# Query and key transposes of two batches moved from TensorE to the DMA crossbar, with paced loads, smaller V loads, a last block in halves and a newly searched plan

## The chip, the cores and the metric

The kernel runs on one core of one Trainium2 chip. The metric is device time in microseconds (us) per execution, as the median of several executions; lower is better. A profile is one execution with every instruction recorded; its span is some 2 us shorter than the time (188.3 against 190.54 us in the kernel before). TensorE (PE) multiplies matrices, VectorE (DVE) and ScalarE (ACT) work element by element, GpSimd (POOL) here makes masks and issues the loads that cast to bf16 ("software" DMA queue), and SyncE (SP) issues all other transfers ("hardware" queue; the page of before has 12896 packets in the one and 43256 in the other).

## The reference

Four batches of attention with eight heads of 64 over 768 positions, each followed by a "wave" layer on the joined heads (512 wide).

```python
# attention: 3 heads causal, 5 "streaming" (4 sink keys and a window of 64)
scores = np.matmul(q, k.transpose(0, 1, 3, 2)) / np.sqrt(D)
a = softmax(np.where(mask, scores, -1e9))
x = np.matmul(a, v)                     # heads joined: [4, 768, 512]
# wave layer
theta = x @ w_theta
y = w_tok_r @ (x * cos(theta)) + w_tok_i @ (x * sin(theta))   # mixes the 768 positions
u = x + y
out = u + np.maximum(u @ w_ch, 0)
```

The kernel lays out every product with its contracted axis on the 128 partitions (the rows of the on-chip memory), so it transposes q and k before the scores, x before theta, and u before the last product. The DMA crossbar, named often below, transposes a block while it is being transferred (DMA_TRANSPOSE in the traces; a block of x, 128x512, lands 2.4 us after issue in the median of before).

## The kernel before

All work is a list of small steps, each with an engine, a duration, what it waits for and which buffer it takes. A scheduler in the kernel plays the list as a plan when the program is built. A step's rank in the plan is corrected by a number from a long list, `TILT`, which a search has tuned; the plan's order is then the fixed order of instructions on each engine. The plan of before already has x (after the first batch) and u (all but the last block) transposed by the DMA crossbar, issued from SP, while q and k are transposed on TensorE:

```python
def turn_qk(what, b, n):                 # 12 transposes of 128x64 into one PSUM bank
    pt = state["pt", what, n] = mine_bf()
    for j in range(NB):
        for x, h in enumerate(PAIRS[n]):
            nc.tensor.transpose(pt[64*x:64*x+64, j*128:(j+1)*128], state[what, b][:, h, j*D:(j+1)*D], ident)

def keep_qk(what, n):                    # the copy out of PSUM, strided, on VectorE or ScalarE
    dst = (qT if what == "q" else kT)[n]
    copy(dst.rearrange("d (p j) -> d p j", j=NB), state.pop(("pt", what, n))[:, :S].rearrange("d (j p) -> d p j", j=NB))

def send_x(b, i):                        # already by crossbar, issued from SP
    nc.sync.dma_start_transpose(state["xT", b][:, :, i*128:(i+1)*128], state["x", b][:, i])
# ... cut: send_u is alike; store, load_v and move_v are plain transfers, also from SP
```

The softmax here doesn't subtract the row's maximum and nothing guards it: scores larger than these inputs give would overflow.

Of the kernel before, what the change touches and what calls it, by code (L numbers as in the profile page):

```python
# [25 lines left out]
    71383, 33577, 73294, -468, 272, 1817, 2121, 1841, 1484, 998, -351, -458, -9998906, -4244, 10993, 53854, -3405,  # L26
    6928, 42937, -27592, 3470, 440, -1170, -8668, 30584, 1187, 131611, 11003, 41350974, 22079, 7061, 59467, 66431,
    42364, 66838, 49232, 30363, 39667, 30343, 71323, 34095, 32360, 33997, 32661, 1599, -643, 481689, -687, 479643,
    10008299, 117742521, 135319420, 117742203, 135320132, 117742437, 135319441, 33665, 30756, 33818, 32757, 33944,
    32167, 96740665, 96740841, 96741207, 96740837, 96740995, -40086, 2489, -29404, 1496, 21511, 2417553, 21872,  # L30
    2417414, 1232, 23224485, 19914, 2417541, 36373805, 2417413, 41478, 20144064, 41910, 7510594, -1006, 10008162,
    27019, 10008687, 2317, -822, 71, 885, 30746, 4782, 28260, -700, 0, 851, 30200, 1234, 16671, -417, 8, -563,
    150, -315, 119, -744, 0, -2086, 0, 548, 3112, 184, 1256, -1791, 0, 218, 752, 196, 3175, -1205, 0, 71357, 6153,
    0, 32543, 49107, 31384, 1227, 34083, 31606, 41910, 2709, 478753, 42322, 1021, 20513511, 10009579, 33487,
    32376, 10009719, 3061386, 20516550, 22990, 135320173, 30384, 2419544, 52082, 68040, 33791, 31401, 59232,
    65497, 71091, 33781, 31241, 33656, 31212, 42036, 19480, 2416926, 79160287, 135318358, 36388668, 9882286,
    36359654, 9867371, 36386091, 9881900, 36360748, 9867822, 36380489, 9885853, 36359579, 16622892, 36360622,
    16626254, 36361168, 16622969, 36361066, 16623202, 4404, 16351, 59586, 28353, 4287, 16466, 36361251, 53261,
    16623326, 16375, 27903, 27573, 27919, 27740, 4295, 4300, 16459, 2029, 29794, 30117, 29643, 30164, 4475, -856,
    24, -2541, 30238, 13762, 8711, 13664, 36359955, 9868033, 53378, 28516, 4917, 16623645, 4811, 16623892, 7, 810,  # L40
    -2223, 740, 30630, 137, 686, 2190, 658, 5916, 2615, 6222, 0, 8869, 3362, -1287, 0, -358, -620, -1072, 378,
    -1088, 358, -1482, 0, -908, 3108, 3053, 2556, 3175, 1994, -541, 4029, -2027, 443, 3087, 6247, 7224, 7707,
    3524, 1446, 145, 28321, -1758, 3046, 3213, 1938, -265, 9029, 2043, 3371, 1753, 3145, 1901, 3091, 5532, 2593,
    3883, -1311, 3122, 3196, 1921, -469, 3313, 2509, -288, 569, 2781, 3713, 9243, 7431, 1470, 0, -192, 3831, 2019,
    0, 952, 2262, 2765, 1417, 4943, 2862, 3017, 627, 4671, 2631, 1041, 6646, 4670, 830, 1866, 27, 4080, 5248,
    5671, 6705, 5103, 5667, 5732, 5378, 7798, 3719, 5937, 5989, 4277, 5669, 5648, 5767, 10067, 15, 5805, 6197,
    3753, 6052, 4214, 4158, 27275, 4065, 3679, 484, 76, 699, 0, 8188, 2442, -2323, 3242, -771, 336, 0, 417, 3878,
    502, 6390, 0, 6397, 0, -201, -390, 2653, -1, 2536, 1439, 0, 27303, 4094, -1220, 699, 571, -377, 0, -2008,
    -550, 489, 1174, 4261, -521, 0, 2334, 3007, 3186, 357, 0, 539, 0, 381, 1594, 769, 681, -1176, 2403, 0, 1644,
    1424, 4167, 4774, -640, 3694, 4115, 1590, 52, 0, 10207, 10302, 17, 5487, 2487, 3322, 3685, 1958, -115, 0,  # L50
    1278, 435, 48, 4630, -7, 1570, 41, 4926, 2732, 2867, 316, -65, 3820, 5940, 46, 5714, -87, 4029, 6008, -900, 0,
    207, 3181, -1890, 0, 372, 425, 2534, 0, 2651, 0, 2938, 7089, 5815, 3035, 4150, -1419, 3038, 4396, -900, 4748,
    3928, 2180, -198, 4640, 4240, -232, 6156, 6885, 5623, 13470, 2411, 1320, 13077, 2453, 2898, 7265, 2931, 3846,
    2887, 7384, 303, 4693, 4266, 2983, 2820, 7808, 332, 2714, 7985, 7738, 3942, 2085, 7081, 13673, 1381, 1001, 97,
    13671, 1776, 2404, 0, 5385, 1277, 2572, 1913, 5381, 904, 2631, 0, 8668, 2704, -145, 1307, 12055, 2019, 142,
    1807, 2720, 2655, 1600, 11967, 4387, 5544, 4391, 5600, 4716, 3728, 2582, 1586, 1908, 1795, 1896, 2095, 3728,
    4504, 11880, 11792, 7607, 1480, 6181, -150, 2513, 3028, 3771, -520, 0, -904, 0, 1201, -1294, 774, 512, 5429,
    1558, 0, 4756, 4685, 3735, -27, 0, 1552, 0, 1212, 347, 0, 2223, 7107, 183, 0, -58, 525, 2032, 6140, 0, -349,
    0, 4456, 229, 3887, 3367, 1689, -826, 0, 13058, 12693, 2337, -246, 1411, -277, 787, 626, -2065, 0, 160, 1199,
    10944, 0, 566, 672, 136, 3705, 10380, 15055, 8015, -17, -1058, 0, 3989, 2971, 1172, 7388, -1070, 0, -401,  # L60
    1423, -2036, 0, 69, 7506, -199, -504, 1956, 8487, 284, 1558, -1901, 622, 1946, 496, 4131, -680, 1961, 7942,
    283, 1343, -1901, 2642, 0, 2935, 2901, -904, 0, 1807, 1884, 661, 0, 1498, 0, 8019, -368, -1831, 6187, 1508,
    13580, 7853, 1348, 13206, 5432, 3571, 1546, 14303, 6167, 1616, 13539, 8035, -553, 887, 6033, 3284, 1481, 8104,
    -515, 7983, -35, 5380, 3520, 4327, 2710, 14882, 4300, -225, 17476, 8037, -229, -2170, 8078, -355, -251, 5364,
    3027, 17524, 37247, 1593, 30869, 0, 37555, 1626, 31594, 0, 22131, 16141, 30282, 0, 21805, 16036, 30305, 41,
    4508, 977, 226, 1349, 2832, 1057, 18, 51, 2854, 2844, 89, 586, 8778, 8244, 8472, 4657, 2899, 2748, -123, -320,
    2283, 2087, 2174, 2098, 1672, 830, -790, -660, 5071, 4133, 3088, 3855, 7423, 7062, 9000, -975, -2753, 3331,
    5493, 1307, 31137, 0, 7964, 7870, 5312, 965, 29975, 54853, 5490, 15749, -619, 0, 587, 9022, 6186, 31738,
    30293, 285, 3736, 15797, -632, 0, 4912, 1715, -342, 1335, -509, 1610, 2359, -3159, -23, 0, 5374, 4362, 4287,
    16854, -304, 53, 2629, 2970, 285, 0, 4350, -993, 1817, 5218, -757, 1251, 2672, -1073, 1792, 0, 2872, 2629,  # L70
    2714, -1232, 767, 0, -1425, 1125, 2390, 0, 4905, 2655, -1663, -651, 2319, 3164, 28456, 141, 20332, 0, 2632,
    2284, -2379, 1034, 2273, 4363, 27747, 1034, 21235, 0, -669, 764, 12072, -454, 19612, 25792, 28797, 881, 21566,
    2456, 28301, 29807, 31171, 921, 30773, 934, 1327, 2527, 20772, 571, 28258, 1526, 1729, 1013, 679, -1128, 2221,
    2979, 21483, 744,
# [3 lines left out]
class Step:  # L78
# [7 lines left out]
    def __init__(self, on, fn, after, take, give, mode, bias, port, share):  # L86
        self.on, self.fn, self.after = on, fn, [a for a in after if a is not None]
        self.take, self.give, self.mode, self.bias, self.port, self.share = take, list(give), mode, bias, port, share
        self.eng = next(iter(on)) if len(on) == 1 else None
        self.users = 0  # L90
        self.slot = self.start = self.end = self.ns = None


class Plan:
# [18 lines left out]
    def add(self, on, ns, fn, after=(), take=None, give=(), mode=None, bias=0, port=False, share=None):  # L113
        s = Step(on if isinstance(on, dict) else {on: ns}, fn, after, take, give, mode, bias, port, share)
        for g in s.give:
            g.users += 1
        self.steps.append(s)
        return s

    def order(self, free):  # L120
# [8 lines left out]
        for s in reversed(self.steps):  # L129
            far = max(self.LATENCY[e][0] for e in s.on)  # L130
            near = min(self.LATENCY[e][1] for e in s.on)
            rank[s.n] = min(s.on.values()) + max((rank[n.n] + (near if len(s.on) == 1 and n.on.keys() == s.on.keys() else far) for n in later[s.n]), default=0)
# [24 lines left out]
        while events:  # L157
# [10 lines left out]
            for e in engines:  # L168
# [34 lines left out]
                if s.share:  # L203
                    o = "DMA" if e == "DMAH" else "DMAH"
                    rest = max(0, free.get(o, 0) - t) + sum(n.on[o] for n in ready.get(o, ()) if ready_at[n.n].get(o, 0) <= t)
                    ns += min(rest, ns * s.share) * (1 - 1 / s.share)
# [5 lines left out]
                far, near = self.LATENCY[e]  # L212
                heapq.heappush(events, (s.end, count, None))
# [19 lines left out]
def kernel(  # L233
# [40 lines left out]
    half_pi = const.tile([128, 1], F32, name="half_pi")  # L274

# [42 lines left out]
    def mine_bf():  # L318
        return mine().bitcast(BF16)
# [41 lines left out]

    def load_v(b, half):
# [627 lines left out]
```

## Time and profile before

| kernel before | |
|---|---|
| time, median of the first three runs | 190.54 us (190.36 to 191.03) |
| profiled span, granted TensorE clock | 188.3 us, 1.00 |
| TensorE busy, of it idle matmuls that fill gaps | 180.1 us, 6.7 us |
| TensorE idle from 0 to 30, 30 to 140, 140 us to the end | 3.8, 0.0, 4.4 us |

The prediction below shows the page and the table by stretches. The columns of a timeline are start, duration, engine and line, operation, destination and source, and how many like it in a row. A duration on SP is the time that SP stands at handing the transfers over, not the transfer: those of x land 2.4 us after issue in the median.

```profile
64.24 2.63 SPq L568 DMA_TRANSPOSE xT<-x  x2
66.96 0.54 SPq L632 DMA_DIRECT2D out_dram<-ot  x1
67.59 4.47 SPq L568 DMA_TRANSPOSE xT<-x  x3
72.11 0.57 SPq L632 DMA_DIRECT2D out_dram<-ot  x1
72.78 1.23 SPq L568 DMA_TRANSPOSE xT<-x  x1
```

These are the six transposes of the second batch's x. One is handed over in 1.2 to 1.5 us, a store in about 0.55, and one follows the other: between 64.24 and 74.01 us SP stands still for less than 0.4 us.

### The profile page before, as it was taken

To read this page: it belongs to the slowest core of one execution; us is meant where nothing else is said; L and a number is where in the kernel's file an instruction comes from. 1 tells how busy PE (TensorE), PEld (TensorE's weight loads), DVE (VectorE), ACT (ScalarE), POOL (GpSimd) and SP (SyncE) were. 2 spreads that over 40 slices of the span, in tenths; PEclk is the share of its full clock that TensorE was granted. 3 is DMA by queue.
4 is the path that set the end of the run, shared out by engine and by line. 5 is a ranking of instruction groups with operands and counts; after the bars stand their busy time and mean duration, and the time that the engine had idled before them with its cause. 6 is when DMAs were issued, how large, how long until landed. Compare 5 with 4: busy or idle time off the path is not lost.

```text
span 188.3 us, 5126 instructions
## 1 busy us (share of the span) xinstructions
PE 180.1 (96%) x2143; PEld 101.2 (54%) x2143; DVE 130.7 (69%) x250; ACT 103.9 (55%) x129; POOL 60.0 (32%) x131
## 2 busy tenths in 40 slices
PE   6699989999999999999999999999999999999982
PEld 6546687764545874454447366444346564444430
DVE  7757696999855986997446466997249259935451
ACT  4488856698777707575780449686860356400010
POOL 7889878109737200005570020500320100000000
PEclk9999999999999999999999999999999999999999
DMA  5999999999999995978999952242344523234323
GB/s 175 173 188 205 200 206 204 208 207 222 147 234 274 196 136 139 209 158 187 181 128 228 104 159 41 61 95 111 87 111 58 168 59 79 61 120 106 108 111 113
DMA packets 56174, 28.06 MB, mean 149 GB/s; under 512 B 40408, under 2 KB 53080, under 8 KB 56152
## 3 DMA queue, kind: packets, MB, share of 16 engines
q1 hardware_dynamic: 43256, 17.65, 43.5%
q0 software_dynamic: 12896, 10.09, 36.1%
q8 instruction: 16, 0.26, 0.6%
q14 instruction: 6, 0.05, 0.1%
HBM read 25.71 MB, written 6.29 MB: 170 GB/s over the span
## 4 chain that ended last, share of the span: by engine, by line
PE 90%; DMA 3%; DVE 3%; ACT 2%; issue 1%; POOL 0%; POOLq 0%
PE bank L602 34%; PE bank L625 12%; PE pair L579 11%; PE pair L462 10%; PE pair L553 9%; PE bank L395 7%; DMA kb<-in_k_dram 3%; PE bank L348 2%; DVE vx L322 2%; PE bank L646 2%; PE bank L615 1%; ACT P L484 1%; PE bank L565 1%; PE pair L529 1%; ACT qT L322 0%
## 5 line engine op out<-in xcount | busy, mean ns | idle before, releaser
L602 PE MATMUL bank<-zr,wtokTr 128*128 128x512 bf16 x144 | 38.7, 380 | 0.0
L602 PE MATMUL bank<-zi,wtokTi 128*128 128x512 bf16 x144 | 38.5, 380 | 0.0
L329 POOL TENSOR_SCALAR_AFFINE_SELECT P<-P 128x256 bf16<-128x256 bf16 (+1 forms) x48 | 16.4, 359 | 45.5 <-ACT P L484 38.4
L606 DVE TENSOR_TENSOR u<-x,bank 128x512 bf16<-128x512 bf16 x24 | 16.5, 686 | 20.1 <-PE bank L602 20.1
L625 PE MATMUL bank<-w_ch_sb,uT 128*128 128x512 bf16 x96 | 24.7, 380 | 0.7 <-ACT uT L322 0.7
L462 PE MATMUL pair<-qT,kT 64*64 64x128 bf16 (+6 forms) x380 | 23.5, 238 | 0.2
L579 PE MATMUL pair<-w_theta_sb,xT 128*128 128x512 bf16 x96 | 23.5, 379 | 0.0
L484 ACT ACTIVATE P<-pair 128x1024 bf16<-128x1024 f32 (+2 forms) x24 | 21.3, 918 | 3.7 <-PE pair L462 3.6
L602 PEld LDWEIGHTS <-wtokTi 128*128 128x128 bf16 x144 | 13.3, 98 | 16.0 <-issue 0.9
L384 POOL COPY kS<-kT 64x4 bf16<-64x4 bf16 x20 | 8.8, 442 | 39.7 <-DVE kT L322 36.8
L462 PEld LDWEIGHTS <-kT 64*64 64x64 bf16 (+1 forms) x380 | 12.3, 102 | 16.2 <-issue 12.0
L602 PEld LDWEIGHTS <-wtokTr 128*128 128x128 bf16 x144 | 12.8, 98 | 15.0 <-issue 1.5
L481 ACT ACTIVATE P_st<-pair 128x1024 bf16<-128x1024 f32 (+1 forms) x16 | 12.7, 810 | 14.1 <-PE pair L462 13.9
L629 DVE SCALAR_TENSOR_TENSOR ot<-bank,u 128x512 f32<-128x512 f32 x24 | 16.4, 689 | 4.8 <-PE bank L625 4.5
L584 ACT ACTIVATE ct<-pair,half_pi 128x1024 f32<-128x1024 f32 x12 | 13.4, 1116 | 7.9 <-PE pair L579 4.6
L560 DVE TENSOR_TENSOR x<-pair,r 128x512 bf16<-128x512 f32 x24 | 16.6, 691 | 0.8
L325 DVE TENSOR_TENSOR zr<-x,ct 128x512 bf16<-128x512 bf16 x24 | 15.9, 688 | 1.7 <-ACT ct L584 1.6
L325 DVE TENSOR_TENSOR zi<-x,st 128x512 bf16<-128x512 bf16 x24 | 15.9, 688 | 0.0
L553 PE MATMUL pair<-vt,P_st 128*128 128x65 bf16 x120 | 14.9, 193 | 0.0
L553 PE MATMUL pair<-vx,P_st 128*128 128x65 bf16 x120 | 14.9, 193 | 0.0
L553 PE MATMUL pair<-vt,P 128*128 128x65 bf16 x252 | 14.1, 194 | 0.7 <-DVE x L560 0.7
L322 ACT COPY uT<-bank 128x512 bf16<-128x512 bf16 x4 | 2.3, 586 | 22.3 <-PE bank L615 22.3
(89 smaller groups left out, 289.7 us busy)
## 6 DMA issues: line engine op xcount, KB each, us to landing
out_dram<-ot SPq DMA_DIRECT2D x24, 256.0 KB, 2.8
v_room<-in_v_dram SPq DMA_DIRECT2D x6, 768.0 KB, 7.4
kb<-in_k_dram POOLq DMA_DIRECT2D x13, 192.0 KB, 5.9
qb<-in_q_dram POOLq DMA_DIRECT2D x13, 192.0 KB, 6.2
wtok<-in_moe_w_tok_r_dram POOLq DMA_DIRECT2D x3, 384.0 KB, 7.2
v_room<-in_v_dram POOLq DMA_DIRECT2D x2, 384.0 KB, 7.4
wtok<-in_moe_w_tok_i_dram POOLq DMA_DIRECT2D x2, 384.0 KB, 7.8
vx<-vt SPq DMA_DIRECT2D x3, 195.0 KB
```

What stands on the lines that cost most here:

```text
L325: {"DVE": nc.vector, "POOL": nc.gpsimd}[state["step"].eng].tensor_tensor(o, a, b, ALU.mult)
L329: nc.gpsimd.affine_select(out=t, in_=t, compare_op=ALU.is_ge, fill=fill, base=base, pattern=pattern, channel_multiplier=cm)
L462: nc.tensor.matmul(ps[half, yy, c:c + w], l, r, start=True, stop=hide is None, skip_group_check=True)
L484: nc.scalar.activation(P.rearrange("p (y c) -> p y c", y=2), ps[:, :, :w0], AF.Exp, scale=scale)
L553: nc.tensor.matmul(o, l, r, start=(m == 0), stop=True, skip_group_check=True)
L560: nc.vector.tensor_tensor(dst, av[:, :, :, :D], r.unsqueeze(3).to_broadcast([128, 2, 4, D]), ALU.mult)
L579: nc.tensor.matmul(ps[:, y], state["xT", b][:, kk, (i + y) * 128:(i + y + 1) * 128], w_theta_sb[:, kk], start=(kk == 0), stop=(kk == KD - 1))
L584: nc.scalar.activation(t, state["th", b, i], AF.Sin, bias=half_pi)
L602: nc.tensor.matmul(py, wtokT[n][:, s, t * 128:(t + 1) * 128], z[:, s], start=(g == 0 and m == 0), stop=(g == 2 and m == 3))
L606: nc.vector.tensor_tensor(u, state["x", b][:, t], state.pop(("py", b, t)), ALU.add)
L625: nc.tensor.matmul(pc, uT[:, kk], w_ch_sb[:, kk], start=(kk == 0), stop=(kk == KD - 1))
L629: nc.vector.scalar_tensor_tensor(ot, state.pop(("pc", b, t)), 0.0, state.pop(("u", b, t)), ALU.max, ALU.add)
```

## The change

The intent is to relieve TensorE, which is full (180.1 of 188.3 us). For batches 3 and 4 a copy on VectorE puts two heads side by side, the crossbar transposes the pair from SBUF to SBUF, and a copy brings it into qT or kT. Loads of q and k for these batches wait for a block of u two batches earlier ("pacing"); V comes in twelve loads in place of six; the last block's work from u on is cut into two halves; and the plan was searched anew, with longer and more frequent DMA delays.

```diff
+    def pair_qk(what, b, n):
+        h0, h1 = PAIRS[n]
+        room = mine()
+        state["qp", what, n] = t = room[:, 0].rearrange("p (j x d) -> p j x d", j=NB, x=2)
+        state["pt", what, n] = room[:, 1]
+        nc.vector.tensor_copy(t, state[what, b][:, h0:h1 + 1:2].rearrange("p x (j d) -> p j x d", d=D))
+
+    def send_qk(what, n):
+        nc.sync.dma_start_transpose(state["pt", what, n].rearrange("p (j t) -> p j t", j=NB), state.pop(("qp", what, n)).rearrange("p j x d -> p (j x d)"))
...
+    BY_DMA = (2, 3)
...
+                if b in BY_DMA:
+                    pair = add("DVE", 330, lambda ...: pair_qk(what, b, n), [landed[what, b, n]], take="wtok", port=True)
+                    tp = add("SP", 1250, lambda ...: send_qk(what, n), [pair])
+                    land = add("DMAH", 900, None, [tp], share=5.2, late=800)
+                    kept[what, b, n] = add({"DVE": 900, "ACT": 1500}, 0, lambda ...: keep_qk(what, n), [land] + old, give=[pair], port=True)
+                    continue
...
-    def load_v(b, half):
-        heads = slice(4 * half, 4 * half + 4)
+    def load_v(b, n):
+        heads = slice(2 * n, 2 * n + 2)
...
+    def paced_load(what, b, n, heads):
+        nc.gpsimd.tensor_copy(pace, state["u", b - 2, n][:1, :1])
+        load_qk(what, b, heads)
...
+        # the last block of the last batch only: make_u_half, turn_u_half, keep_u_half,
+        # channel_half, finish_half, store_half, each twice with 256 of the 512 columns
...
 TILT = [      # all 854 numbers replaced by 905 others
```

## The prediction

> **What bounds the kernel now.** I read the page first (busy shares, then the 40 slices), then the chain of waits that ended last, then the busy table by stretches of ten microseconds, and last the timeline of the end. All lines are of the kernel before.
>
> ```profile
> span 188.3 us, 5126 instructions
> PE 180.1 (96%) x2143; PEld 101.2 (54%) x2143; DVE 130.7 (69%) x250; ACT 103.9 (55%) x129; POOL 60.0 (32%) x131
> ...
> PE   6699989999999999999999999999999999999982
> ...
> DMA  5999999999999995978999952242344523234323
> ...
> PE 90%; DMA 3%; DVE 3%; ACT 2%; issue 1%; POOL 0%; POOLq 0%
> ```
>
> TensorE is busy for 180.1 of 188.3 us, and the chain that sets the end lies on it for 90%. The digits of the slices show where it is not full: about the first six slices and the last two. The DMA row is full up to slice 23 (about 105 us) and a third full after that. The table by stretches sharpens this:
>
> ```profile
> core 0: us, PE busy (x) PEld busy (x) DVE busy (x) ACT busy (x) POOL busy (x), PEclk, DMA share, GB/s
> 0.00:10.00 10.00, 6.92 (x109) 6.07 (x109) 7.26 (x30) 4.63 (x6) 8.32 (x24) 1.00 0.97 176
> ...
> 70.00:80.00 10.00, 10.00 (x65) 4.63 (x63) 8.39 (x16) 5.67 (x6) 0.00 (x0) 1.00 0.82 172
> 80.00:90.00 10.00, 10.00 (x98) 5.22 (x93) 8.25 (x13) 6.72 (x9) 3.01 (x8) 1.00 0.83 176
> ...
> 110.00:120.00 10.00, 10.00 (x137) 5.94 (x136) 7.10 (x14) 5.63 (x8) 2.07 (x5) 1.00 0.37 81
> 120.00:130.00 10.00, 10.00 (x104) 4.65 (x101) 9.18 (x16) 8.53 (x10) 1.03 (x2) 1.00 0.39 111
> ```
>
> From 30 to 180 us TensorE is busy 10.00 us in every ten, at a granted clock of 1.00. In that stretch whatever leaves TensorE shortens the kernel, as long as the other engines keep it fed, and nothing else does. Of its 180.1 us, 6.7 are 72 idle matmuls of the first 30 us (line 948), which fill gaps; real work is 180.1 - 6.7 = 173.4 us, and 188.3 - 173.4 = 14.9 us are start, end and a few gaps.
>
> [...] In the trace a single transpose is 219 ns, but twelve of 128x64 pass in a row in 0.34 to 0.46 us, while a crossbar transpose of four 128x128 blocks (xT) takes 2.4 us from issue to landing. So the crossbar is much the slower path; its merit is only that it is not TensorE. [...] the mean DMA share in a stretch, summed over the two queues, reaches 1.34 while q and k load. [...] before has 34 transposes, all issued from SP, and the change issues its own from SP too[...]. [...] The trace has 956 ns for a strided 128x768 copy out of PSUM (kT, qT) and 556 ns for a plain one (wtok), and no strided 128x768 copy within SBUF.
>
> **The change, part by part.**
>
> *1. Transposes of q and k in the third and fourth batch leave TensorE.* Two batches of eight tiles of twelve transposes: 192 of the 384. In the chain they stand at 58.86, 79.59, 84.06, 92.24, 108.89, 116.07, 119.89 and 124.29 us, in pieces of 24, 36, 12, 24, 24, 36, 12 and 24:
>
> ```profile
> 79.59 1.13 PE bank L395 x36
> ...
> 84.06 0.46 PE bank L395 x12
> ...
> 92.24 0.79 PE bank L395 x24
> ```
>
> Summed: 4 x 0.79 + 2 x 1.13 + 2 x 0.46 = 6.34 us. From 12 (0.46) to 36 (1.13) the slope is 0.028 us each, so 192 x 0.028 = 5.4 us of streaming[...]. All of it lies in the full stretch, on the path. [...] I take -6.0 us, between 5.4 and 6.3.
>
> *2. What replaces them.* 16 pairings on VectorE (128x768 bf16 within SBUF; the diff reckons 330 ns each[...]): +5.3 us. 16 issues on the SP queue at 1.2 us (the median of the xT issues): +19 us on a queue that holds 34 of them. 16 crossbar transfers of 192 KB; the diff reckons 0.9 us each when undisturbed, +14 us. 16 final copies on VectorE or ScalarE as before, but the diff reckons 900 ns on VectorE and 1500 on ScalarE from SBUF, where ScalarE took 800 ns from PSUM. About seven of the 16 are now on ScalarE; if all go to VectorE, it gains 7 x 0.9 = 6.3 us and ScalarE loses 5.6. VectorE: 130.7 + 5.3 + 6.3 = 142 of about 182 us, 78%. Nothing of this is on the path by itself, but it raises the chance that TensorE waits.
>
> *3. V by two heads.* Six loads of 768 KB, 7.4 us to landing, become twelve of 384 KB; the same bytes and the same twelve casts (562 ns). Casts begin earlier. TensorE waits for no V in the stretch from 30 us on, so I give it 0. *Paced loads*: 16 tiny copies on GpSimd, each making a load of batch 3 or 4 wait for a block of u two batches earlier. GpSimd is idle in most of 60 to 125 us; 0 on the path, and the DMA load moves later. *The search*: another order of the same work; 0 by itself.
>
> *4. The last block in halves.* The end of the timeline:
>
> ```profile
> 181.75 0.69 DVE L606 TENSOR_TENSOR u<-x,bank 128x512 bf16<-128x512 bf16 x1 [1.03 <-PE bank L602]
> ...
> 182.93 0.59 ACT L322 COPY uT<-bank 128x512 bf16<-128x512 bf16 x1 [20.04 <-PE bank L615]
> 183.57 0.55 PEld L625 LDWEIGHTS <-uT 128*128 128x128 bf16 x4 [0.85 <-ACT uT L322]
> 183.57 1.04 PE L625 MATMUL bank<-w_ch_sb,uT 128*128 128x512 bf16 x4 [0.68 <-ACT uT L322]
> 184.65 0.69 DVE L629 SCALAR_TENSOR_TENSOR ot<-bank,u 128x512 f32<-128x512 f32 x1 [1.34 <-PE bank L625]
> ```
>
> From 181.75 to the final product's start at 183.57 are 1.82 us in series. In halves the second half of u (an estimate of 0.42 us for 256 columns, from 0.69 for 512 and 0.29 for 256 in the masks) passes beside the first transposes and copy: about 0.3 us less. The last element-wise step is 0.42 instead of 0.69: 0.27 less. The store behind it is half as large; of the 188.3 - 185.34 = 2.96 us most is latency, say 0.1 to 0.2 less. Sum -0.7 us.
>
> *Sum.* 188.3 - 6.0 - 0.7 = 181.6 us of span. The median time lies 190.54 - 188.3 = 2.24 us above the profiled span; that gives 183.8. To this I add 1.2 us of new gaps on TensorE, a judgement rather than a count: a saturated TensorE that is relieved of 3% leaves the others that much less slack, and a plan that expects late DMA puts safe work where better work would stand. Predicted: 185.0 us.
>
> **The rivals.**
>
> *VectorE becomes the bound in the attention stages.* From 70 to 90 and from 120 to 130 us it is already at 8.2 to 9.2 of 10, and that is just where pairs and final copies must go. For: in the 60 us from 70 to 130 it is busy 44.1; with 11.6 more and TensorE's share 5.5 shorter it would be 55.7 of 54.5. Against: a pairing can be done any time after its load lands and before the transposes were due, and from 130 us on VectorE is busy only about 5 to 7 of 10, so other work can slide. If it binds, half of the gain goes: 187 to 188 us.
>
> *The crossbar's latency takes the place of the removed work.* Pairing 0.35, issue and landing 2.4 or more, copy 0.9 is about 4 us, where a transpose and its copy were 1.4; the pairs share four buffers and the SP queue runs in order, so one late block of x or u holds up all behind it. For: the DMA share is 0.82 and 0.83 from 70 to 90 us. Against: from 105 us it is 0.3 to 0.5, the pacing takes load out of the crowded part, and the plan was searched with late DMA. If it binds for the third batch only: 2 to 3 us, 186 to 187 us.
>
> *TensorE only moves its idle time*, if the start (14.9 us of non-work minus the end) grew with the new order: 0 to 2 us. And the other way: a fresh search may tighten the first 30 us, where 6.7 us of idle matmuls stand; that would give 182 to 183.
>
> **Range and chances.** The floor is the sum without gaps, 183.8, less about 1 us for a better start: 182.8. The ceiling is the VectorE rival with half a microsecond of bad start: 188.5. Faster by over 2% means below 186.7; the centre is 1.7 us under it, so 0.70. Slower by over 2% needs 194.4, which would take new gaps of 10 us: 0.03.
>
> **What would show it.** Right: line 395's matmuls at 192 instead of 384, TensorE's real work near 167 us and still 10.00 of 10 between 35 and 175 us, VectorE near 140 us, and the last copy, product and store in halves with some 0.7 us less from the last u to the end. Wrong: the stretch table with TensorE under 9.5 anywhere from 60 to 130 us, with waits of the score matmuls for kT or qT copies (VectorE or crossbar behind them, which the releaser tells apart); or a longer start before the first mixing product at 41.3 us. If final copies within SBUF take about half of 0.9 us, the VectorE rival falls and the time is near 184.

The sum came to 188.3 - 6.0 - 0.7 + 2.24 + 1.2 = 185.0 us. In part 1 the -6.0 is between the 5.4 us of the slope and the 6.34 of the chain.

## The result

The changed kernel took 197.96 us in the median of four runs (197.08, 197.95 and 197.98 in the fast state, 202.02 in the slow one), the kernel before 190.78 in the same rounds (190.36 to 191.28). The ratio is 1.036, 95% interval 1.031 to 1.041: slower, where 185.0 us was predicted. A ratio is the mean time of one kernel's fast runs over that of the other's fast runs of the same rounds, so not quite the ratio of the medians quoted.

The page of the changed kernel, the rows that answer to those of before:

```profile
span 195.4 us, 4859 instructions
PE 179.3 (92%) x1962; PEld 98.9 (51%) x1962; DVE 132.5 (68%) x267; ACT 109.9 (56%) x131; POOL 61.5 (31%) x147
...
PE   6799999989999937999999999759999999999991
...
PEclk9789999999999995899999999999999999999999
...
PE 65%; DVE 15%; DMA 14%; issue 3%; POOL 1%; DVEq 0%; ACT 0%; SPq 0%
```

TensorE's row has holes where it was full: the 15th and 16th of the 40 slices (68 to 78 us) and the 26th and 27th (122 to 132 us). Its share of the ending chain fell from 90 to 65%, and VectorE and DMA took 29%. The granted clock is low in the second and third slice and in the 16th and 17th. The stretches (columns as in the prediction):

```profile
70.00:80.00 10.00, 5.69 (x42) 3.14 (x42) 4.29 (x10) 3.27 (x4) 0.00 (x0) 0.66 0.89 162
...
120.00:130.00 10.00, 8.02 (x64) 3.68 (x61) 6.58 (x13) 6.90 (x6) 0.00 (x0) 1.00 0.69 157
130.00:140.00 10.00, 8.78 (x74) 3.51 (x76) 9.65 (x17) 9.20 (x9) 1.49 (x6) 1.00 0.56 142
```

From 70 to 80 us TensorE was busy for 5.69 us, and at a mean clock of 0.66. TensorE's account over the whole span, before against after:

| part of the span | before | after | difference |
|---|---|---|---|
| idle, 30 to 140 us | 0.0 | 8.6 | +8.6 |
| idle, start (0 to 30) and end (from 140) | 8.2 | 7.5 | -0.7 |
| idle matmuls that fill gaps | 6.7 | 8.0 | +1.3 |
| all other matmuls | 173.4 | 171.3 | -2.1 |
| sum | 188.3 | 195.4 | +7.1 |

The -2.1 us are the removed transposes (6.3 us by the prediction's count of chain pieces) less what half clock cost. The stretch from 7.7 to 11.1 us has 3.40 us of work at clock 0.50 and that from 72.3 to 79.2 us 4.72 at 0.52; half of that, about 4.1 us, was lost to the clock (an estimate: in the chain four matmuls of theta took 1.89 us after the gap and 1.60 in a row in the second stretch, and take 1.04 and 0.86 at a clock of 1.00). So some 6.3 us of work did go, and 8.6 us of waiting and 4.1 of half clock came. (1.11 us of the early stretch are filling matmuls, so 0.55 of the 4.1 is also in the +1.3; the account is no finer than half a microsecond.) The early half clock has no tie to the change that a run shows: a_no_pace and a_late_pairs below have 1.00 in the first 20 us.

Where the waiting comes from is in the chain that ended last, in order of time (start, us, what), around the first hole and after it:

```profile
63.57 4.73 DMA out_dram<-ot
...
69.51 4.92 DMA xT<-x
...
74.47 1.89 PE pair L591 x4
...
97.25 4.80 DMA uT<-u
...
122.09 3.12 DMA wtok<-wtok
...
128.73 2.45 DMA xT<-x
```

TensorE's own timeline has the same hole, with the idle time before the matmuls in brackets:

```profile
74.47 1.89 PE L591 MATMUL pair<-w_theta_sb,xT 128*128 128x512 bf16 x4 [4.31 <-DMA xT<-x]
```

The hole at 70 us ends when a transpose of x lands, at 74.43. Not the new transposes (wtok) but the old ones come late there. SP's timeline says why:

```profile
52.67 6.68 SPq L365 DMA_DIRECT2D v_room<-in_v_dram  x3
59.46 4.06 SPq L411 DMA_TRANSPOSE wtok<-wtok  x1
63.57 0.96 SPq L679 DMA_DIRECT2D out_dram<-ot  x1
64.69 1.35 SPq L411 DMA_TRANSPOSE wtok<-wtok  x1
66.15 1.34 SPq L580 DMA_TRANSPOSE xT<-x  x1
67.53 1.88 SPq L389 DMA_DIRECT2D vs_f<-in_v_dram  x5
69.51 4.91 SPq L580 DMA_TRANSPOSE xT<-x  x3
```

VectorE had finished three blocks of x by 62.67 us. SP had three loads of V until 59.35, then the first new transpose until 63.52 (4.06 us for one, not 1.2; the profile does not tell why), then a store and a second new one; it reached the first of these blocks of x at 66.15 and the next at 69.51. In this timeline SP takes one transfer after the other, so the transposes of x stood behind the new ones.

That this is SP's queue and not the whole program can be read from the kernel's own plan, which gives a start for each step. The lag of the trace behind the plan, worked out step by step, in us:

| step | plan | lag in the trace |
|---|---|---|
| before: normalising x, second batch | 59.9 to 64.9 | 3.2 to 3.3 |
| before: transposes of this x on SP | 60.9 to 66.4 | 3.3 to 4.5 |
| after: normalising x, second batch, first four | 55.1 to 59.8 | 3.6 to 3.9 |
| after: transposes of this x on SP | 56.4 to 61.7 | 9.7 to 11.6 |
| after: normalising x, the last two | 68.1, 71.0 | 10.0, 10.6 |
| after: third batch, fifth and sixth block | 107.5, 111.3 | 12.1, 15.1 |

SP fell 6 to 8 us behind VectorE, and then all engines took over that lag; around 110 us it happened again. At the end the lag is 16 us, against 5.8 in the kernel before.

Not all of SP's lag comes from the new transposes. SP was 3.1 us behind its plan at the first of the three loads of V (52.67 against 49.6), 6.0 at the first new transpose (59.46 against 53.5) and 8.9 at the store after it (63.57 against 54.7). So the loads of V, which the new plan puts just there, have a share in this hole; b_pace_v below clears them only in the order of before. And the transpose of x handed over at 69.51 took 4.92 us to land, twice the 2.4 of before, so late landing is a part of the hole too.

The groups of the new and changed operations (busy us, mean ns, idle before):

```profile
L408 DVE COPY wtok<-kb 128x768 bf16<-128x768 bf16 x8 | 3.1, 396 | 0.3 <-DMA kb<-in_k_dram 0.3
L324 DVE COPY kT<-wtok 128x768 bf16<-128x768 bf16 x4 | 3.3, 821 | 0.0
L324 ACT COPY kT<-wtok 128x768 bf16<-128x768 bf16 x4 | 6.1, 1516 | 1.5 <-DMA wtok<-wtok 1.5
L976 POOL COPY pace<-u 1x1 bf16<-1x1 bf16 x16 | 4.6, 286 | 7.0 <-DVE u L618 6.0 <-DVE r L570 1.1
```

A pairing took about 0.37 us, the final copy from SBUF 0.82 us on VectorE and 1.5 on ScalarE (0.96 and 0.80 from PSUM). None is far from the plan, and VectorE ends at 132.5 us, not at the 142 reckoned.

The end, in the timeline:

```profile
188.66 0.75 DVE L649 TENSOR_TENSOR u<-x,bank 128x256 bf16<-128x256 bf16 x2 [0.17 <-PE bank L614]
...
190.22 1.10 PE L666 MATMUL bank<-w_ch_sb,uT 128*128 128x256 bf16 x8 [0.46 <-ACT uT L324]
191.36 0.76 DVE L672 SCALAR_TENSOR_TENSOR ot<-bank,u 128x256 f32<-128x256 f32 x2 [1.15 <-PE bank L666]
```

From the last u to the product are 1.56 us against 1.82 before. But both last copies run after both halves of the product, in 0.76 us together against 0.69 for the one of before; from the last u to the end are 6.74 us against 6.55. The smaller stores gave nothing here: from the last copy to the end are 3.28 us, and 2.96 before.

### The profile page after: what moved, and what is told of

Same layout as the page of the kernel before. It is cut to its first block, busy times and chain, and to the rows that moved or that the text cites. A ratio compares the mean times of both kernels' runs of the same rounds, so it can differ in the third digit from the quotient of the medians.

```text
span 195.4 us, 4859 instructions
## 1 busy us (share of the span) xinstructions
PE 179.3 (92%) x1962; PEld 98.9 (51%) x1962; DVE 132.5 (68%) x267; ACT 109.9 (56%) x131; POOL 61.5 (31%) x147
## 4 chain that ended last, share of the span: by engine, by line
PE 65%; DVE 15%; DMA 14%; issue 3%; POOL 1%; DVEq 0%; ACT 0%; SPq 0%
PE bank L614 23%; PE pair L591 9%; PE pair L565 9%; PE pair L474 7%; PE bank L637 7%; DMA xT<-x 4%; DMA qb<-in_q_dram 3%; PE bank L396 3%; DMA uT<-u 2%; DMA out_dram<-ot 2%; DVE zi L327 2%; DVE zr L327 2%; PE bank L350 2%; PE bank L1027 2%; DVE u L618 2%
## 5 line engine op out<-in xcount | busy, mean ns | idle before, releaser
L591 PE MATMUL pair<-w_theta_sb,xT 128*128 128x512 bf16 x96 | 25.3, 399 | 7.4 <-DMA xT<-x 5.9
L474 PE MATMUL pair<-qT,kT 64*64 64x128 bf16 (+6 forms) x380 | 24.5, 240 | 0.0
L331 POOL TENSOR_SCALAR_AFFINE_SELECT P<-P 128x256 bf16<-128x256 bf16 (+1 forms) x48 | 17.1, 383 | 22.4 <-ACT P L496 14.7
L637 PE MATMUL bank<-w_ch_sb,uT 128*128 128x512 bf16 x92 | 23.4, 380 | 0.3 <-DMA uT<-u 0.2
L385 POOL COPY kS<-kT 64x4 bf16<-64x4 bf16 x20 | 6.1, 305 | 54.7 <-ACT kT L324 30.9
L618 DVE TENSOR_TENSOR u<-x,bank 128x512 bf16<-128x512 bf16 x23 | 15.8, 686 | 11.0 <-PE bank L614 10.6
L641 DVE SCALAR_TENSOR_TENSOR ot<-bank,u 128x512 f32<-128x512 f32 x23 | 15.8, 688 | 4.7 <-PE bank L637 4.0
L591 PEld LDWEIGHTS <-xT 128*128 128x128 bf16 x96 | 9.2, 101 | 18.9 <-DMA xT<-x 8.3
L327 DVE TENSOR_TENSOR zr<-x,ct 128x512 bf16<-128x512 bf16 x24 | 15.7, 686 | 0.7 <-ACT ct L596 0.7
L327 DVE TENSOR_TENSOR zi<-x,st 128x512 bf16<-128x512 bf16 x24 | 15.7, 687 | 0.0
L565 PEld LDWEIGHTS <-P 128*128 128x128 bf16 x252 | 12.7, 100 | 4.4 <-issue 0.9
```

What stands on the lines that cost most here:

```text
L327: {"DVE": nc.vector, "POOL": nc.gpsimd}[state["step"].eng].tensor_tensor(o, a, b, ALU.mult)
L331: nc.gpsimd.affine_select(out=t, in_=t, compare_op=ALU.is_ge, fill=fill, base=base, pattern=pattern, channel_multiplier=cm)
L474: nc.tensor.matmul(ps[half, yy, c:c + w], l, r, start=True, stop=hide is None, skip_group_check=True)
L565: nc.tensor.matmul(o, l, r, start=(m == 0), stop=True, skip_group_check=True)
L591: nc.tensor.matmul(ps[:, y], state["xT", b][:, kk, (i + y) * 128:(i + y + 1) * 128], w_theta_sb[:, kk], start=(kk == 0), stop=(kk == KD - 1))
L618: nc.vector.tensor_tensor(u, state["x", b][:, t], state.pop(("py", b, t)), ALU.add)
```

## The experiments

The expectations name their theories. *Blocked queues*: VectorE, ScalarE and SP stand in order behind one late transfer. *Crowded DMA*: the DMA engines have more to move (the hardware queue took 43.5% of the 16 engines' 188.3 us before and 50.0% of 195.4 after, 15.8 us more of all engines, or about 1 us for each of the 16 new transfers). *Backlog*, from the second round (b_cross4) on: each crossbar transfer put in before the last load moves the end of all loading. That a new order costs by itself was first tested late, in x_before; a_undo then weighs Theory A, the crossbar, against Theory B, the order alone. "After" is the changed kernel; names with a_ are made from it, names with b_ keep before's order, and names with x_ have an order that I searched with a model of the plan under transfers 12 to 25% longer. All ratios are against the kernel before on the same chip, fast runs alone; slow is here a run over 1.5% above the fastest of its kernel. Within a kernel the fast runs differ by 1 to 2%, so the intervals matter more than the medians.

### Single parts, and one blockage

**a_no_pace**: after without the 16 pacing copies.

```diff
-        nc.gpsimd.tensor_copy(pace, state["u", b - 2, n][:1, :1])
```

> The changed kernel in its own order, only the sixteen tiny GpSimd copies that pace the loads of q and k are taken out (GpSimd waited 6.0 us for u in them). My theory (blocked queues): the loss comes from VectorE, ScalarE and SP standing in order behind a transfer that lands later than the plan reckoned, so loads issued up to 3.5 us sooner shorten the first stall only in part; 1 to 4 us less than the changed kernel's 197.9, so 194 to 197, and the gap on TensorE near 70 us (4.3 us) becomes shorter[...]. Rival (crowded DMA): nothing gained or a loss, since the loads then collide with V and the weights: 197 to 200. Rival (pacing is the fault): most of the 7 us comes back, below 192.

Measured: 197.50 us, ratio 1.030 (1.017 to 1.043). Pacing is not the cause; TensorE is still idle for 3.5 us from 70 to 80 us, against 4.3 in after.

**a_late_pairs**: after, but the two pairings and issues that stood in front of the x of the first hole (k and q, first pair of the third batch) go behind the fourth block of that x.

```diff
+    for m, key in enumerate(((2, "k", 0), (2, "q", 0))):
+        pair, send = crossed[key]
+        pair.start = norm[1, 3].start + 1 + m
+        send.start = <start of send_x of the fourth block> + 1 + m
```

> The changed kernel, only the first two pairings of batch 3 and their two crossbar issues are moved behind the fourth normalisation and the fourth crossbar issue of x of batch 2; bytes, number of transfers and everything else as before. Blocked queues: VectorE no longer waits 3.4 us for the q and k loads and SP no longer stands still from 59.5 to 63.5 us with the rows of x behind it, so the 4.3 us gap on TensorE near 70 us and the half clock after it (6.8 us at half) mostly go: 190 to 193. Crowded DMA: the same traffic, so no change within 1%: 196 to 199.

Measured: 197.84 us, ratio 1.034 (1.021 to 1.047). The two issues were indeed in the way: the idle time from 70 to 80 us fell from 4.3 to 2.8 us. The time did not change, as crowded DMA had it (196 to 199) and not blocked queues (190 to 193): later waits took the place of this one. The chain of this kernel, in order of time:

```profile
112.19 7.44 DMA xT<-x
```

One transpose of x took 7.44 us to land, with TensorE idle behind it for 2.7 us in this stretch of ten. Taking away one blockage shows the next.

**b_halves**: before with the last block's six steps each done in two halves.

```diff
+    for s, fn in tail:      # make_u, turn_u, keep_u, channel, finish, store of the last block
+        s.fn = lambda fn=fn: [fn(B - 1, NB - 1, x) for x in range(2)]
```

> The kernel before in its own order, only the last block in halves. Prediction of part 4: 0.7 us less, between 0.3 and 1.0, so 189.8 to 190.3 where the kernel before has 190.6. In the profile of the changed kernel the time from the last u to the start of the last product was 1.56 us where it was 1.82. Rival: the two stores follow each other on the SP queue and nothing is gained at the end: 190.4 to 190.8.

Measured: 193.44 us in the median, with two slow runs of four; the fast runs give 1.002 (0.986 to 1.018). Its profile has 1.56 us from the last u to the product (181.84 to 183.40) and both last copies behind both halves of it, as in after. The saved quarter of a microsecond is lost again at the copies, so this part gains nothing within the scatter.

**b_pace_v**: pacing and V in twelve loads, in before's order.

```diff
+        for m in (2 * half, 2 * half + 1):
+            heads = slice(2 * m, 2 * m + 2)
...
+        nc.gpsimd.tensor_copy(pace, state["u", b - 2, n][:1, :1])
```

> Part 3 alone in the order of before: the loads of q and k of batches 3 and 4 wait for u as in the change, V comes in twelve loads of 384 KB in place of six of 768 KB; all transposes on TensorE, casts as before. Prediction: 0 us, so 190 to 191.5. If this part carries a share of the loss (loads later, into the time of x and u; six more issues on SP): 192 to 195.

Measured: 190.85 us against 190.78, ratio 1.001 (0.994 to 1.008). These two parts cost and gain nothing, as predicted.

### The crossbar alone, in before's order

**b_cross**: batches 3 and 4 by crossbar in before's order, each pairing 6 us before its final copy.

```diff
+    at = keep.start - 6000          # for all 16 tiles; the 192 transposes on TensorE dropped
+    order += [pair at `at`, send at `at` + 330]
```

> The kernel before in its own order, unpaced and with V in halves, only the transposes of q and k of batches 3 and 4 go through the crossbar: pairing and issue stand 6 us ahead of the final copy, whose place and engine are kept. Blocked queues: the crossbar as such is harmless when it is started early enough; TensorE loses 192 transposes (6 us), some of it given back in waits for copies that are twice as long on ScalarE: 185 to 189. Crowded DMA: sixteen more crossbar transfers (some 16 us of all engines) make loads, x and u late: 191 to 197.

Measured: a wrong result (relative error 0.0435), 211.65 us and slow. The first pairings took buffers that still held token-mixing weights. No conclusion is drawn from it.

**b_cross4**: the same for batch 4 only, where the buffers are free; correct.

```diff
-    BY_DMA = (2, 3)
+    BY_DMA = (3,)
```

> The first runs moved the lag behind the plan at 72 us (from +11 to +9), yet at 118 us it was +15 to +16 all the same, when the backlog of transfers ended. New theory (backlog): up to the last q and k load the 16 DMA engines have hardly a gap, so each crossbar transfer put in there (about 1 us of all engines) moves the end of the backlog, and with it xT, uT and qT, by its own length; after it the crossbar is free. Kernel before, only batch 4 through the crossbar, pairing 6 us ahead of the final copy, so nearly all transfers come after 104 us, behind the last load. Backlog: TensorE loses 96 transposes (3 us), little comes back: 187.0 to 189.5 where before has 190.7. Blocked queues (VectorE, ScalarE and SP standing in order behind crossbar landings, whenever they are): half the loss of the changed kernel or more, 192 to 195.

Measured: 195.87 us, ratio 1.023 (1.017 to 1.029). Half of the crossbar, in the order of before, already loses, which the backlog theory had not expected (187.0 to 189.5). Its stretches (those of before stand at 10.00):

```profile
110.00:120.00 10.00, 8.20 (x102) 4.68 (x101) 7.63 (x17) 7.56 (x8) 1.76 (x5) 1.00 0.76 148
120.00:130.00 10.00, 7.25 (x30) 2.88 (x31) 6.20 (x13) 6.06 (x6) 1.49 (x5) 0.83 0.68 142
```

TensorE is busy for 10.00 of 10 us in each stretch from 30 to 100 us, and loses 6.3 us between 100 and 140, where the crossbar is used, at a mean DMA share of only 0.7 in the worst two stretches.

**b_cross4_lead**: the same with 10 us of lead, not before 100 us.

```diff
-    at = keep.start - 6000
+    at = max(keep.start - 10000, 100000)
```

> b_cross4 with the pairings 10 us ahead of the final copies instead of 6, though not before 100 us of the plan, so that landings come well before the copies on VectorE and ScalarE. Blocked copies as the main cause of b_cross4's loss (2.8 us of VectorE waiting for one landing lies in its chain): 188 to 192. Transfers of x and u late behind the crossbar's on the one hardware queue: no better than b_cross4's 195.9, or worse, 195 to 198.

Measured: 196.35 us, ratio 1.029 (1.023 to 1.035). More time for the landing didn't help, so the latency of the new transposes themselves is not what costs.

**b_cross34**: batch 4 and six of the eight tiles of batch 3 (those after 75 us).

```diff
+    crossed = [c for c in crossed if c[4].start > 75000]
```

> As b_cross4, with six of the eight tiles of batch 3 through the crossbar too, only those whose final copy the plan has after 75 us (by then the four buffers no longer hold weights, which b_cross overwrote). Backlog: six transfers more in the stretch before 106 us, so the last q and k load lands some 4 to 6 us later; 190 to 195, slower than b_cross4 by 2 to 6 us in spite of 2.3 us less on TensorE. If the crossbar is harmless when started early: 185.5 to 188.

Measured: 202.76 us, ratio 1.060 (1.050 to 1.069), correct. With before's order the second batch costs still more.

### What of the crossbar costs

**b_traffic**: before, with 13 more crossbar transposes of 192 KB on SP at the places where after has its own. Nothing waits for them.

```diff
+    nc.sync.dma_start_transpose(buffers["wtok"][n % 4][:, 1].rearrange("p (j t) -> p j t", j=NB), m_stream)
+    # at 66.3, 68.3, 70.8, 74.6, 78.8, 91.9, ... 114.3 us of the plan
```

> The kernel before with all its TensorE transposes, plus 13 crossbar transfers of 192 KB from a constant tile into buffers that nobody reads, issued on SP where the changed kernel has its own after 66 us. No compute engine waits for them. Backlog: the end of the backlog moves from 106 us to 113 to 119 us and xT and uT land 5 to 10 us after issue as in the changed kernel; 196 to 203. Blocked queues: only SP's issue time, 190.5 to 193.

Measured: 196.09 us, ratio 1.026 (1.020 to 1.032). Transfers that nobody needs cost 5 us by being there. This is what I had expected of the backlog (196 to 203); for blocked queues I had expected only 190.5 to 193. The next two runs decide against the backlog.

**b_traffic_late**: the same 13 at 122 to 146 us, where the DMA share is 0.3 to 0.5 in before.

> The same 13 transfers, issued between 122 and 146 us of the plan, behind the last load, where the DMA share is 0.3 to 0.5. Both theories: no more than 1.5 us of loss, 190.5 to 192.2; if SP's issue time or the crossbar itself hurt anywhere, this would be as slow as b_traffic.

Measured: 196.33 us, ratio 1.023 (1.013 to 1.033); the fast runs reach from 194.07 to 196.53. My expectation fell: it had the cost tied to the busy stretch of DMA. In the trace the transposes of the fourth batch's x start 6.6 to 13 us behind the plan, the normalising of the first five blocks only 5.0 to 5.4: they stand behind the dummies on SP. The DMA share there is 0.75 from 140 to 150 us and 0.88 from 150 to 160, against 1.2 to 1.3 while the loads run.

**b_traffic_small**: the 13 of b_traffic with 32 KB in place of 192.

```diff
-    ...buffers["wtok"][n % 4][:, 1].rearrange("p (j t) -> p j t", j=NB), m_stream)
+    ...buffers["wtok"][n % 4][:, 1, :128], m_stream[:, :128])
```

> b_traffic with the same 13 issues at the same places on SP, but each transfer moves one block of 128x128 (32 KB) in place of six (192 KB). If the loss of b_traffic (5 us) is bytes on the DMA engines: a sixth of it, 190.5 to 192. If it is the issue time and the order on SP (13 issues of 1.2 us or more in front of x, u and stores): most of it stays, 193.5 to 196.

Measured: 197.58 us, ratio 1.032 (1.024 to 1.040). A sixth of the bytes, and the time is no shorter. The profile needs care: its first transpose of x starts at 67.35 us, 3.1 us later than in before (64.24) and ahead of the first dummy (74.09), so only some 4.5 us of its loss come after that; in b_traffic it is 6.7. Handing over one took 1.2 us in the median, as against 1.3 for the large ones. So most of the cost goes not with the bytes but with the 13 issues. That SP's own time is all of it is not shown: the small dummies still took 4.3 us in the median to land, the transposes of x 3.5 (2.4 in before) and one u in the chain 8.79, so what is queued behind SP is slow as well.

**b_stores_pool** and **a_stores_pool**: the output stores issued by GpSimd, in before (24) and after (23), to relieve SP.

```diff
-        nc.sync.dma_start(out=out[b, t * 128:(t + 1) * 128, :], in_=...)
+        nc.gpsimd.dma_start(out=out[b, t * 128:(t + 1) * 128, :], in_=...)
```

> The same alone in the kernel before. If before is near the edge of the SP queue too (in its profile one issue takes 4.67 us and transfers of u land after 6 us while q and k load): 188.5 to 190.5, a little faster. If SP is not near the edge in before: 190.0 to 192.

> The changed kernel in its own order, only the 23 whole stores of the output are issued by GpSimd (which is idle after 115 us) in place of SP, so SP has 23 issues of about 0.55 us less and a store no longer stands in front of a crossbar transfer on the hardware queue, nor waits behind one. SP order (one queue in order carries x, u, q, k, V and stores): 1 to 5 us less than the changed kernel's 197.9, 193 to 197. Bytes on the DMA engines: the same bytes, 197 to 199.

Measured: 194.62 us, ratio 1.018 (1.011 to 1.026), and 200.81 us, ratio 1.048 (1.038 to 1.058). Both are slower than their base, so the relief that I hoped for did not show. Handing over a store takes GpSimd 0.55 us, about as long as SP, but GpSimd stands 63.6 us in all (in b_stores_pool) waiting for results to store, with loads and masks in order behind them. Whether the idea or GpSimd failed is left open; it takes nothing from the tests above and adds nothing.

### The order alone, and the order with the crossbar

**x_before**: the steps of before, unchanged, in an order that I searched on a model.

```diff
 TILT = [      # 854 other numbers, nothing else
```

> The steps of before without any change, only another order, searched here in the same way as x_none and x_four (the model says 2.4 us less than before's own order when transfers are 12 to 25% longer). It tells what a new order costs by itself. If x_none and x_four lost their 4 us through their parts: 189 to 191. If the order of before is adapted to the chip and any other one that only a model has proved loses: 193 to 196, as x_none and x_four.

Measured: 194.89 us, ratio 1.020 (1.011 to 1.029). No work was changed; this modelled order costs 2% by itself, although the model had it 2.4 us faster. Why the order of before does better on the chip is not shown.

**x_none**, **x_four**, **x_both**: all parts of the change, with no batch, with batch 4, and with batches 3 and 4 by crossbar, each with its own searched order.

```diff
-    BY_DMA = (2, 3)
+    BY_DMA = ()        # x_none;   (3,) in x_four;   (2, 3) in x_both
```

> Everything of the change except the crossbar for q and k: paced loads, V by two heads, last block in halves, and an order of its own (searched here by running each order with all transfers 12% and 25% longer, since the old one does not fit a changed list of steps). TensorE transposes all q and k again. Backlog (crossbar transfers are what makes the rest late): 189.5 to 193.5, near before. If pacing, V or the halves make the loss: 195 or more, as the changed kernel.

> As x_none, but batch 4 alone goes through the crossbar, with an order searched in the same way, so that its transfers and those of x and u are not reckoned with too little time. Backlog: behind the last load the crossbar has room, TensorE loses 3 us: 186 to 190, faster than before by up to 2%. Blocked queues as the main cause: the copies wait again, 192 to 196, as b_cross4.

> All steps of the changed kernel, both batches by crossbar, but in an order searched anew on a model with all transfers 12 to 25% longer (the same procedure as the kernels with no batch and with one batch by crossbar, which gave 1.022 and 1.022). If what costs is the particular order of the changed kernel, this one is at theirs or better, TensorE having 6 us less work than in the first: 192 to 195 us, ratio 1.00 to 1.02. If a second batch by crossbar costs on SP and in landings what it saves on TensorE, whatever the order: 195 to 199 us, ratio 1.02 to 1.045.

Measured: x_none 195.38 us, ratio 1.022 (1.014 to 1.030); x_four 195.26 us, ratio 1.022 (1.017 to 1.028); x_both 202.42 us, with three slow runs of six; the fast ones give 1.047 (1.039 to 1.056). One batch by crossbar saves TensorE 3.1 us and brings nothing; the second, in yet another searched order, brings a loss of 2.5% more.

**a_undo**: after's own order with the crossbar taken out: pairings and issues dropped, the 192 transposes on TensorE 0.7 us before each final copy.

```diff
+    order = [s for s in order if s is no pairing and no send of q or k]
+    order.append(turn_qk at keep.start - 700, in a PSUM bank that is free)
```

> The changed kernel with only the crossbar undone: its 16 pairings, 16 issues and 16 crossbar transfers are taken out, and the 192 transposes stand again on TensorE, about 0.7 us before each final copy, at the place of that copy in the changed kernel's order (two copies move by less than 0.7 us; everything else keeps its place). TensorE gets 6.3 us of work back. Theory A, it is the crossbar (its issues on SP and its late landings): the 4 us gap at 70 us and the waits of 110 to 130 us go, and the time is that of the kernel before, 190 to 193 us, ratio 0.99 to 1.01. Theory B, it is the new order alone, which was tried on no chip: the waits for xT and uT stay and 6 us of work are added, 197 to 202 us, ratio 1.03 to 1.05. Both by halves: 194 to 196, ratio 1.015 to 1.03.

Measured: the profiled run took 616 us, an accident in which each matmul of 512 columns took 1.07 to 1.10 us (0.38 in after; means of one), at a recorded clock of 1.00; it is of no use here, so this kernel has no profile. Of the other five, two were fast (195.18 and 195.83) and three slow (199.24 to 200.16). The ratio of the fast runs is 1.025 (1.018 to 1.033), on two runs only. That is what I had written for both theories by halves: the order alone costs 2 to 3%, and with the crossbar, which takes 6 us off TensorE, it costs 3.6%. The intervals touch, and the three slow runs of a_undo are slower than the fast ones of after, so I take it only as this: in after's order the crossbar gains nothing.

### The runs side by side

| order | q and k not by crossbar | batch 4 | batches 3 and 4 |
|---|---|---|---|
| of before | 1.000 (b_pace_v 1.001) | 1.023 (b_cross4) | 1.060 (b_cross34, 14 tiles of 16) |
| of after | 1.025 (a_undo) | none | 1.036 (after) |
| searched here | 1.020 (x_before), 1.022 (x_none) | 1.022 (x_four) | 1.047 (x_both) |

In every row the time rises or stays from left to right, although TensorE loses 3 us of work at each step. TensorE's idle time in the two stages where batches 3 and 4 have their q and k turned shows where (one profile each; some records are missing, 1962 weight loads and 1939 matmuls in a_late_pairs, so a microsecond means little):

| idle of TensorE, us | 60 to 100 | 100 to 140 |
|---|---|---|
| before, b_pace_v, x_none (no crossbar) | 0.0, 1.1, 1.7 | 0.0, 0.6, 0.0 |
| x_before (no crossbar) | 0.8 | 3.1 |
| b_cross4, x_four (batch 4) | 0.0, 0.4 | 6.3, 3.4 |
| after, b_cross34, x_both (batches 3 and 4) | 4.4, 6.4, 5.6 | 3.4, 6.0, 4.9 |

Where batch 3 goes by crossbar, TensorE idles for 4 to 6 us in the first stage, and otherwise for less than 2. Where batch 4 does, it idles for 3 to 6 us in the second, and in the other kernels of the table for less than 1, except for x_before, where it waits for one uT (2.5 us). Each batch trades 3.1 us of transposes for more than 3 us of waiting. What ends these waits is mostly the landing of an old transpose: of x for 5.9 us in after, of x and u for 3.3 and 1.1 in b_cross4, of u for 2.6 in b_traffic_small.

No kernel tried beat the one before.

## Why the prediction was wrong

*Part 1, -6.0 us of transposes: right.* 192 remain, and in the groups they are busy for 8.4 us, where 384 were for 15.7. In the account above, 6.3 us of removed work is what makes the busy time agree.

*Part 2, "Nothing of this is on the path by itself": the step that failed.* I weighed the 19 us of issues against SP's count of 34 transposes, as a load, and not against the moments at which SP has to be free. Two things were missed. The old transposes of x and u, on which TensorE waits within a few microseconds, use the same queue, which took them in order (the x at 66.15 and 69.51 after the new ones at 59.46 and 64.69); and an issue isn't always 1.2 us (4.06 us at 59.46). Both signs were in the profile of before: SP stands for 4.67 us at one transfer at 76.10, and transposes of u took up to 6.5 us to land. The runs put 8.6 us of idle TensorE in its place. b_traffic shows the cost without any dependence on the transfers, b_traffic_small that it is mostly not the bytes, b_traffic_late that it isn't tied to the crowded DMA stretch, and b_cross4_lead that it isn't the new transposes' own latency. Two things stay open: how the cost divides between SP's time and late landings behind it, and how much a queue of its own for x and u would give back, as the attempt with the stores settled nothing and issuing x and u, or the new transposes, from an engine other than SP was not tried.

*The 1.2 us for new gaps: mis-sized.* The term measured 8.6 us from 30 to 140 us, and with it half clock: about 2.4 us of lost work after the hole at 70 us. In the hole an idle time of 4.31 us before 74.47 is followed by four matmuls in 1.89 us, where 1.04 is usual at full clock (at 131.22). No length of gap that decides it shows in the runs: the clock was at 0.50 for 3.4 us after a gap of 1.29 us (after, from 7.7 us) and after one of 1.82 (b_traffic, from 95.3), in x_before it was 0.93 and 0.89 from 100 to 120 us, where the longest wait was 2.5, and it stayed at 1.00 after gaps of 1.53 (before, at 6.95) and 2.62 (b_traffic_small, at 110.5). What makes it fall is not shown. I had no term for it. The gap and the clock after it, in b_traffic and then in b_traffic_small (in the stretches the clock is the third figure from the end):

```profile
94.96 1.58 PE L602 MATMUL bank<-zr,wtokTr 128*128 128x512 bf16 x4 [1.82 <-DVE ot L629]
95.30:98.70 3.40, 3.40 (x27) 1.17 (x25) 1.61 (x3) 1.57 (x2) 1.54 (x6) 0.50 1.32 185
...
110.51 1.04 PE L625 MATMUL bank<-w_ch_sb,uT 128*128 128x512 bf16 x4 [2.62 <-DMA uT<-u]
110.60:114.00 3.40, 3.40 (x29) 1.32 (x30) 1.12 (x2) 1.29 (x2) 0.00 (x0) 1.00 0.43 87
```

*Part 3, pacing and V: right at 0* (b_pace_v 1.001). *"The search: another order of the same work; 0 by itself": wrong.* x_before is the test: same steps, another modelled order, +2.0%. a_undo gives 2.5% for the order of the change itself. So of the 3.6% more than half goes with the order, and the rest is what the crossbar costs beyond the 6 us that it saves. This split rests on two fast runs of a_undo and is no finer than a per cent.

*Part 4, -0.7 us: wrong.* The start of the product came 0.26 us earlier, as the step of 0.3 has it. But the second element-wise half did not pass beside the product's second half: both ran after it, in 0.76 us, and 0.19 us more passed to the end. Why they wait for both halves no run settles.

*Sum.* 188.3 - 6.3 (transposes) + 8.6 (waits in the middle) - 0.7 (waits at the ends) + 1.3 (filling matmuls) + 4.1 (half clock) = 195.3, and 195.4 was measured; 0.55 us of it is counted twice, and 1.7 us is the early half clock, which I cannot lay to the change.

*The rivals.* VectorE as the bound: fell, it ends at 132.5 us; the final copies take 0.82 us on VectorE (0.96 from PSUM before) and seven of sixteen stayed on ScalarE. The crossbar's latency: the right place, with the wrong direction and size. I wrote that one late block of x or u would hold up the transposes of q and k. It was mostly the other way round: those held up x and u (one new landing, 3.12 us at 122.09, is in the chain as well), and it cost not 2 to 3 us but what the account shows. I set it aside with DMA shares of 0.3 to 0.5 from 105 us, and b_cross4 stalled at 0.7, so that share was the wrong measure. The signs I named did their work: the stretch table fell below 9.5 between 60 and 130 us, but the waits were theta's for xT, not the scores' for kT or qT.

## What to carry to other kernels

Before you move work from a full engine to a DMA queue, read the timeline of the issuing engine and not only the DMA share: count who else on that queue is needed within a few microseconds, and test it with the same transfers as dummies that nobody waits for. A schedule can be worth something itself (2% here, x_before), so a change that comes with a fresh, only modelled schedule should be judged against the old work in a fresh schedule as well. In a saturated kernel a gap on TensorE can cost more than itself: the one of 4.31 us in after was followed by 4.72 us of work at a clock of 0.52 and one of 1.82 us in b_traffic by 3.40 at 0.50, though one of 2.62 us in b_traffic_small by none.
